# Fetching four more weight pieces and the second group's inputs in the first burst, and reordering VectorE's part of the first chain

## Chip, cores and metric

The kernel runs on one core of a Trainium2 chip. The metric is the device time of one execution in microseconds (us). A core has TensorE (PE, matrix multiply, with its weight loads shown as PEld), VectorE (DVE), ScalarE (ACT), GpSimd (POOL) and SyncE (SP), which here issues every DMA transfer.

## What is computed

Two stages follow each other. The first is a delta rule, token by token, for 4 x 8 heads of 768 tokens of size 48; the second a gated MLP on the 3072 rows that come out of it, each of 384 numbers, with 1536 hidden units:

```python
for t in range(S):
    kt, vt, bt = (k_n[:, :, t], v[:, :, t], beta[:, :, t, None])
    y[:, :, t] = np.einsum('bhd,bhde->bhe', q[:, :, t], state)
    v_old = np.einsum('bhde,bhd->bhe', state, kt)
    state = state + bt[:, :, :, None] * np.einsum('bhd,bhe->bhde', kt, vt - v_old)
...
gate = 1.0 / (1.0 + np.exp(-(x @ w_gate)))
val = x @ w_val
return (gate * val @ w_out).astype(np.float32)
```

The rows of k are normalised to length one first (k_n). The weights come as doubles, so each of their numbers arrives as two 32-bit words.

## The kernel before

The 768 tokens are cut into 12 groups of 64 tokens. For a group all 32 heads are worked at once: products of the keys among themselves (`gram`), a triangular solve by VectorE (`norms`, then `solve` or `solve_halves`), the group's share of the state (`rest`, `updates`, `advance`), masked products of keys and queries (`masked`), and the group's rows of y (`rows`), turned so that they can go into the MLP (`flip`, later `turn`). The MLP of a group is 12 tiles of 128 hidden units: `gate_val`, `gated`, `outp`. The MLP of one group runs while the delta rule of the next is prepared, in slots whose order a hand-written plan sets: the order in which instructions are written is the order in which each engine runs its own.

The first group has no MLP to run beside. Its work stands in lines 667 to 726 and is called the first chain here: on VectorE the norms of group 0, a solve in two halves of 16 steps (39 steps of `halves0`), then 11 steps of `norms1` while TensorE and ScalarE join the halves, the last two steps (the second ends in the subtraction of line 430, kept as `joint`), and then `updates(0, 0)`, `updates(0, 1)`, `updates(0, 2)`, `rows(0)` and `flip`. An `updates` step is 64 small matmuls (line 477, or 469 for the middle step) and copies out of PSUM by ScalarE (line 483) and VectorE (line 481), or two subtractions on VectorE (line 457) in the middle step. Between them `busy_array` puts filling matmuls. The first MLP matmul (line 583) is the first of slot 0.

The weights are 36 pieces of 384 KB. `load_piece` issues one (line 172); ScalarE turns the words of a piece in two passes (`scaled`, lines 189 and 191); VectorE joins them (`join`, line 203). Fourteen pieces (EAGER) are asked for by hand with `stage`: ten right away, pieces 10 and 11 once `joint` is done, 12 and 13 once ScalarE has done `lower_left(1)`. From then on `scaled(n)` asks for piece n + BEHIND when it is done. The same places also hold the loads of group 1's queries (`load_q(1)`, two transfers of 256 KB), of its keys by token (`load_rows(1, 0)`, 384 KB), and of the keys of group 2 (`load_k(2)`, two of 192 KB), whose buffer is free after the matmuls of `masked(0)`.

SP issues in the order written, and an issue that has to wait holds all behind it. Transfers complete on eight counters used in turn, so an issue also waits until the transfer eight before it has landed; at most eight are under way.

`masks0` are four VectorE multiplications (line 324) that mask the first group's query products for `rows(0)`; `halves1` is the solve of group 1, whose first four steps (lines 383 and 386) set it up; `joins` are the joins of the pieces in order.

Of the kernel before, what the change touches and what calls it, by code (L numbers as in the profile page):

```python
# [36 lines left out]
def tokens_at(e, x):  # L37
    return 64 * e if x else 64 - 64 * e
# [17 lines left out]
def deltanet_gated_mlp(ctx: ExitStack, tc: tile.TileContext, kd, qd, kv, beta, words, out):  # L56
# [27 lines left out]
    state = [{} for _ in range(N)]  # L84

    def pace(ins, after):
        if after is not None:
            tc.add_manual_dep(ins.ins, after.ins.name, mybir.DependencyInfo(mybir.DependencyClass.Sync, mybir.DependencyReason.DATA), reason="pace")
# [7 lines left out]
    def busy_array(out, n, after=()):  # L96

        for i in range(n):
            ins = nc.tensor.matmul(out=out.rearrange("q a b -> q (a b)"), lhsT=flat[:, 0:128], rhs=flat, start=True, stop=True)
            if i < len(after):  # L100
                pace(ins, after[i])

    def load_k(g):
        for e in range(2):
            nc.sync.dma_start(kqp[g % 2][64 * e:64 * e + D, 0:2].rearrange("p s c t -> p (s c t)"), kd[g, e])

    def load_q(g, after=None):
        for e in range(2):
            ins = nc.sync.dma_start(kqp[g % 2][64 * e:64 * e + 64, 2 + e:4 + e].rearrange("p s c t -> p (s c t)"), qd[g, e])
            pace(ins, after)  # L110

    def load_rows(g, part):

        st = state[g]
        if "kv" not in st:
            st["kv"] = wk.tile([128, 2, CP, D], F32, name=f"kv_{g}", tag="kv", bufs=2)
        nc.sync.dma_start(st["kv"][:, part].rearrange("p c d -> p (c d)"), kv[g, :, part * CP * D:(part + 1) * CP * D])
        if part:
            st["beta"] = wk.tile([128, 32], F32, name=f"beta_{g}", tag="beta", bufs=2)
            nc.sync.dma_start(st["beta"], beta[:, g])  # L120
# [48 lines left out]
    def load_piece(n, after=None):  # L169
        f, w = pieces[n]  # L170
        raw[n] = wt.tile([128, PW, 2], U32, name=f"raw_{n}", tag=f"w{n}")
        ins = nc.sync.dma_start(raw[n].rearrange("p c w -> p (c w)"), words[3 * f + "gvo".index(w)])
        pace(ins, after)

    def stage(lo, hi, after=None):
        for n in range(lo, hi):
            load_piece(n, after)
# [43 lines left out]
    def joining():  # L221
        for n in range(len(pieces)):
            join(n)
            yield

    def splitting():
        for n in range(len(pieces) + 1):
            if n:
                weight_lo(n - 1)
            if n < len(pieces):  # L230
                weight_hi(n)
            yield
# [78 lines left out]
    def masked(g):  # L311

        kq = kqp[g % 2]
        pool, tag = (ps_aux, "aux") if g else (ps_out, "po")
        pp = [pool.tile([128, J, C], F32, name=f"pp_{g}_{e}", tag=tag) for e in range(2)]
        for j in range(J):
            for e, x in KINDS:
                r, t = 64 * e, tokens_at(e, x)
                nc.tensor.matmul(out=pp[e][t:t + 64, j], lhsT=kq[r:r + D, x, j], rhs=kq[r:r + D, 3 if x else 2 + 2 * e, j], start=True, stop=True)  # L319

        def masks():
            for e, x in sorted(KINDS):
                t, sec = tokens_at(e, x), 5 if x else 2 + 2 * e
                nc.vector.tensor_tensor(out=kq[t:t + 64, sec], in0=pp[e][t:t + 64],  # L324
                                        in1=pmask[t:t + 64, e].unsqueeze(1).to_broadcast([64, J, C]), op=ALU.mult)
                yield
        return masks()
# [27 lines left out]
    def lower_left(g):  # L355

        if g == 0:
            for r in range(4):
                q, o = slice(32 * r, 32 * r + 32), 32 * (r % 2)
                nc.scalar.activation(wide[q, :, o:o + 16].rearrange("q c t -> q t c"), state[g]["G"][q, 0:16], AF.Copy, scale=under[q])  # L360
            return
        a = joints[g][:, 0]
        return nc.scalar.activation(a[:, :, 0:16].rearrange("q c t -> q t c"), state[g]["G"][:, 0:16], AF.Copy, scale=under)
# [5 lines left out]
    def clear(g):  # L369
        state[g]["X"] = X = wk.tile([128, 16, 32], F32, name=f"X_{g}", tag="X", bufs=1)  # L370
        nc.gpsimd.memset(X, 0.0)
# [62 lines left out]
    def rest(g):  # L434

        st = state[g]
        kq, V = kqp[g % 2], st["kv"][:, 1]
        st["pk"] = pk = [ps_seq.tile([128, J, D], F32, name=f"pk_{g}_{e}", tag="seq") for e in range(2)]
        if g == 0:
            for e in range(2):  # L440
                nc.tensor.matmul(out=pk[e].rearrange("q j d -> q (j d)"), lhsT=flat[:, 0:128], rhs=su[:, 2].rearrange("q j d -> q (j d)").bitcast(BF16)[:, 0:J * D],
                                 start=True, stop=True, skip_group_check=True)
        for j in range(J if g else 0):
            for e, x in KINDS:
                r, t = 64 * e, tokens_at(e, x)
                nc.tensor.matmul(out=pk[e][t:t + 64, j], lhsT=kq[r:r + D, x, j], rhs=su[r:r + D, 2 if x else e, j],  # L446
                                 start=j == 0, stop=True, skip_group_check=True)
        if g == 0:
            st["R"] = [V[:, e * J:(e + 1) * J] for e in range(2)]
        else:  # L450
            st["R"] = [wk.tile([128, J, D], F32, name=f"R_{g}_{e}", tag="row", bufs=3) for e in range(2)]
            less(g)

    def less(g):
        st = state[g]
        for e in range(2):
            nc.vector.tensor_tensor(out=st["R"][e], in0=st["kv"][:, 1, e * J:(e + 1) * J], in1=st["pk"][e], op=ALU.subtract)  # L457

    def updates(g, step):

        st = state[g]
        R, L = st["R"], st["L"]

        at = {(e, x): [tokens_at(e, x) + 32 * (k ^ e) for k in range(2)] for e, x in KINDS}
        if step == 1:
            for j in range(J):
                for e, x in KINDS:
                    one, two = at[e, x]
                    nc.tensor.matmul(out=st["pk"][e][two:two + 32, j], lhsT=L[one:one + 32, e * J + j], rhs=su[one:one + 32, 3 if x else e, j],  # L469
                                     start=False, stop=True, skip_group_check=True)  # L470
            less(g)
            return
        pu = [ps_aux.tile([128, J, D], F32, name=f"pu_{g}_{step}_{x}", tag="aux") for x in range(1 if g else 2)]
        for j in range(J):
            for e, x in KINDS:
                r = at[e, x][step // 2]
                nc.tensor.matmul(out=pu[0 if g else x][r:r + 32, j], lhsT=mt[r:r + 32, e * J + j], rhs=R[e][r:r + 32, j], start=True, stop=True)  # L477
        for e, x in KINDS:
            r = at[e, x][step // 2]
            if g == 0 and x:  # L480
                nc.vector.tensor_copy(out=su[r:r + 32, 3 if x else e], in_=pu[1][r:r + 32])
            else:
                nc.scalar.copy(su[r:r + 32, 3 if x else e], pu[0][r:r + 32])  # L483
# [168 lines left out]
    def take(gen, n=1):  # L652
        for _ in range(n):
            next(gen, None)
# [5 lines left out]
    scalings = [scale_v(g) for g in range(N)]  # L660
    NORMS, SOLVE, HALVES = 18, 66, 40
    joins, splits = joining(), splitting()
    EAGER, BEHIND = 14, 6


    EN = mybir.EngineType
# [6 lines left out]
    stage(3, 6)  # L673
    load_rows(0, 0)
    load_rows(1, 1)
    stage(6, 10)
    half = constants()
    clear(0)
    take(gram(0), 10)
    rest(0)  # L680
    masks0 = masked(0)
    gap.append(ps_gv.tile([128, J, C], F32, name="early", tag="gv"))
    busy_array(gap.pop(), 12)
    for n in range(2):
# [7 lines left out]
    halves0, norms1, halves1 = solve_halves(0), norms(1), solve_halves(1)  # L692
# [2 lines left out]
        scaled(n)  # L695
    take(norms1, 11)
    take(halves0, 2)
    stage(10, 12, state[0]["joint"])
    load_q(1, state[0]["joint"])
    clear(1)  # L700
    take(masks0, 2)
    updates(0, 0)
    busy_array(gap[0], 5)
    stage(12, 14, lower_left(1))
    load_rows(1, 0)
    load_k(2)
    for n in range(6, 9):
        scaled(n)
    take(masks0, 2)
    updates(0, 1)  # L710
    busy_array(gap[0], 4)
    take(norms1, NORMS)
    updates(0, 2)
    busy_array(gap[0], 5)
    for n in range(9, 11):
        scaled(n)
    take(joins, 2)
    take(halves1, 4)
    rows(0)
    busy_array(gap[0], 2)  # L720
    for n in range(11, 13):
# [6 lines left out]
    for n, at in enumerate((0, 0, 1, 2, 3, 5, 6, 8, 9, 10, 10, 11, 11, 12, 12, 13, 14, 15, 16, 16, 17, 18, 18), 13):  # L728
        plan[at].append(lambda n=n: scaled(n))
    spread(joins, len(pieces) - 4, 0, 20)  # L730
    for at, n in ((0, 8), (1, 4), (2, 6), (3, 4), (4, 5), (5, 5), (6, 1), (9, 1), (11, 1)):
        plan[at].append(steps(halves1, n))
    plan[10].insert(0, steps(halves1))
    late[10].append(steps(halves1))
# [147 lines left out]
```

## Time and profile before

| what | value |
|---|---|
| median of 3 runs | 637.5 us (637.04 to 637.57) |
| the profiled execution | 635.61 us |
| its span, first to last instruction | 633.9 us |
| TensorE busy | 614.6 us (97%) |
| VectorE busy | 476.8 us (75%) |
| ScalarE busy | 344.0 us (54%) |
| start of the first MLP matmul | 42.09 us |

The profiled execution lies 1.9 us below the median of the runs, and 1.7 us of it lie outside its span. All times of rows are counted from the span's start. On the page, the chain of work that ended last says which engine sets the end, and the timelines say when each piece ran; a wait that the trace ties to nothing is called "issue".

### The profile page before, as it was taken

How to read it: one execution, taken by the hardware profiler on the slowest of the kernel's cores; microseconds unless marked ns; L12 is line 12 of the kernel's file. 1: busy time of each engine (PE TensorE's matmuls, PEld its weight loads, DVE VectorE, ACT ScalarE, POOL GpSimd, SP SyncE). 2: the span in 40 equal slices, each digit the busy share in tenths (PEclk: the TensorE clock that was granted, in tenths of full speed). 3: DMA queues.
4: the chain of work that ended last, by engine and by line, in shares of the span. 5: the costliest groups of instructions: out<-in, count | busy, mean ns of one | idle time of the engine just before them, and what ended most of it. 6: DMA issues, size and time to landing. Idle time of an engine off the chain costs nothing.

```text
span 633.9 us, 24057 instructions
## 1 busy us (share of the span) xinstructions
PE 614.6 (97%) x10494; PEld 571.2 (90%) x10502; DVE 476.8 (75%) x1443; ACT 344.0 (54%) x933; POOL 39.6 (6%) x102
## 2 busy tenths in 40 slices
PE   6689999999999999999999999999999999999996
PEld 4367778989999999999999999999999999999996
DVE  5888897589977977977977977977987977953221
ACT  4879865567356356356355355355455455445222
POOL 6000000000002002002002002002002002001000
PEclk9999999999999999999999999999999999999999
DMA  9495831202203203103102102102112100100101
GB/s 271 177 296 181 277 91 54 53 2 87 52 3 86 52 4 86 42 12 86 45 11 86 34 21 87 27 28 86 26 29 86 26 4 3 26 3 2 26 1 25
DMA packets 17769, 41.06 MB, mean 65 GB/s; under 512 B 4224, under 2 KB 7296, under 8 KB 17664
## 3 DMA queue, kind: packets, MB, share of 16 engines
q1 hardware_dynamic: 17664, 39.53, 21.5%
q8 instruction: 82, 1.34, 0.9%
q14 instruction: 23, 0.19, 0.1%
HBM read 34.80 MB, written 4.72 MB: 62 GB/s over the span
## 4 chain that ended last, share of the span: by engine, by line
PE 91%; DVE 5%; ACT 1%; issue 1%; DMA 1%; ACTq 0%; SPq 0%; DVEq 0%
PE gv L586 45%; PE po L617 22%; PE gv L583 5%; PE pu L477 3%; PE po L611 3%; PE yy L503 2%; PE yy L506 2%; PE pk L446 2%; PE pg L291 2%; PE pp L319 2%; PE pd L524 2%; PE pk L469 1%; PE pm L409 1%; ACT su L483 1%; DVE kqp L324 1%
## 5 line engine op out<-in xcount | busy, mean ns | idle before, releaser
L586 PE MATMUL gv<-xx,w 128*128 128x256 f32 x2376 | 311.2, 285 | 0.0
L586 PEld LDWEIGHTS gv<-xx,w 128*128 128x128 f32 x2376 | 298.8, 191 | 3.1
L617 PE MATMUL po<-w,h 128*128 128x384 f32 x792 | 161.9, 340 | 0.0
L617 PEld LDWEIGHTS po<-w,h 128*128 128x128 f32 x792 | 133.8, 188 | 0.8
L597 ACT CAST h<-sg 128x256 fp32r<-128x256 f32 x132 | 53.5, 405 | 120.1 <-DVE sg L592 119.0
L591 ACT ACTIVATE sg<-gv 128x256 f32<-128x256 f32 x144 | 54.7, 380 | 107.8 <-PE gv L586 98.5
L592 DVE TENSOR_TENSOR sg<-sg,gv 128x256 f32<-128x256 f32 x144 | 60.1, 417 | 67.3 <-ACT sg L591 66.5
L350 DVE TENSOR_TENSOR X<-X,tmp 128x126 f32<-128x126 f32 (+22 forms) x279 | 71.1, 255 | 8.3
L347 DVE TENSOR_TENSOR tmp<-X,gp 128x126 f32<-128x126 f32 (+22 forms) x279 | 71.0, 254 | 8.3
L602 DVE TENSOR_TENSOR h<-sg,h 128x256 fp32r<-128x256 f32 x132 | 56.4, 428 | 13.2 <-ACT h L597 13.2
L562 POOL COPY x<-yt 32x192 f32<-32x192 f32 x72 | 28.3, 393 | 450.3 <-DVE yt L557 447.6
L279 ACT ACTIVATE kv<-kv,mq 128x48 f32<-128x48 f32 x192 | 47.9, 324 | 0.0
L483 ACT COPY su<-pu 32x384 f32<-32x384 f32 x92 | 43.3, 470 | 5.9 <-PE pu L477 4.1
L583 PE MATMUL gv<-xx,u 128*128 128x256 f32 x144 | 33.8, 385 | 0.7 <-issue 0.4
L324 DVE TENSOR_TENSOR kqp<-pp,pmask 64x512 f32<-64x512 f32 x48 | 32.3, 687 | 2.1 <-PE pp L319 1.1
L303 ACT COPY G<-pg 32x256 f32<-32x256 f32 (+1 forms) x69 | 25.3, 367 | 14.0 <-PE pg L291 12.7
L583 PEld LDWEIGHTS gv<-xx,u 128*128 128x128 f32 x144 | 26.6, 190 | 5.8 <-issue 0.8
L557 DVE STREAM_TRANSPOSE yt<-ys 128x768 f32<-128x768 f32 x9 | 8.8, 979 | 25.4 <-ACT ys L512 25.4
L457 DVE TENSOR_TENSOR R<-kv,pk 128x384 f32<-128x384 f32 x44 | 22.3, 549 | 6.6 <-PE pk L469 6.5
L562 ACT COPY x<-yt 32x192 f32<-32x192 f32 x72 | 25.2, 349 | 1.2
L212 ACT CAST w<-u 128x384 fp32r<-128x384 f32 x36 | 18.0, 508 | 8.1 <-DVE w L219 8.0
L531 DVE TENSOR_TENSOR su<-su,pd 48x384 f32<-48x384 f32 x40 | 21.7, 543 | 0.8 <-PE pd L524 0.4
(109 smaller groups left out, 556.2 us busy)
## 6 DMA issues: line engine op xcount, KB each, us to landing
raw<-in_words_dram SPq DMA_DIRECT2D x36, 384.0 KB, 5.5
kv<-in_kv_dram SPq DMA_DIRECT2D x24, 384.0 KB, 4.5
kqp<-in_qd_dram SPq DMA_DIRECT2D x24, 256.0 KB, 4.1
kqp<-in_kd_dram SPq DMA_DIRECT2D x24, 192.0 KB, 3.5
out_dram<-ot SPq DMA_DIRECT2D x48, 96.0 KB, 2.2
beta<-in_beta_dram SPq DMA_DIRECT2D x12, 16.0 KB, 4.0
```

The lines of the kernel that those rows point to most:

```text
L279: nc.scalar.activation(V[:, c], V[:, c], AF.Copy, scale=mq[:, c, 0:1])
L347: nc.vector.tensor_tensor(out=tmp, in0=X[:, k:16, j:j + 1].to_broadcast([128, n, j]), in1=gp[:, j:j + 1, 0:j].to_broadcast([128, n, j]), o ...
L350: nc.vector.tensor_tensor(out=X[:, k:16, 0:j], in0=X[:, k:16, 0:j], in1=tmp, op=ALU.add)
L483: nc.scalar.copy(su[r:r + 32, 3 if x else e], pu[0][r:r + 32])
L562: copy(x[32 * q:32 * q + 32, :, :, a].rearrange("q k c s -> q c k s"), yt[32 * a:32 * a + 32, :, q::4])
L583: nc.tensor.matmul(out=pg[:, o], lhsT=parts[w, f][:, k * 128:(k + 1) * 128], rhs=x[0][:, k], start=k == 0, stop=k == KC - 1)
L586: nc.tensor.matmul(out=pg[:, o], lhsT=parts[w, f][:, a, k * 128:(k + 1) * 128], rhs=x[b][:, k], start=(k == 0 and q == 0), stop=(k == KC - ...
L591: nc.scalar.activation(h, st["gv", f][:, 0], AF.Sigmoid)
L592: nc.vector.tensor_tensor(out=h, in0=h, in1=st["gv", f][:, 1], op=ALU.mult)
L597: nc.scalar.copy(hh[:, 0], st["sg", f])
L602: nc.vector.tensor_tensor(out=hh[:, 1], in0=st["sg", f], in1=hh[:, 0].bitcast(F32), op=ALU.subtract)
L617: nc.tensor.matmul(out=po[s], lhsT=hh[:, a, ts], rhs=parts["o", f][:, w], start=(f == 0 and q == 0), stop=(f == NF - 1 and q == 2))
```

## The change

- Pieces 10 to 13, the queries of group 1 and its keys by token are asked for right behind the first ten pieces, with no wait for `joint` or `lower_left(1)`; the keys of group 2 right behind `masked(0)`.
- BEHIND falls from 6 to 5: `scaled(n)` asks for piece n + 5, so piece 14 is asked for by `scaled(9)`, no longer by `scaled(8)`.
- The first two joins move from before `rows(0)` to before `updates(0, 0)`.
- The last two masks move from before `updates(0, 1)` to behind it.
- The last seven steps of `norms1` move from before `updates(0, 2)` to behind it.
- The first four steps of `halves1` move from before `rows(0)` into slots 1 to 3.

```diff
--- before.py
+++ after.py
@@ -660,7 +660,7 @@
     scalings = [scale_v(g) for g in range(N)]
     NORMS, SOLVE, HALVES = 18, 66, 40
     joins, splits = joining(), splitting()
-    EAGER, BEHIND = 14, 6
+    EAGER, BEHIND = 14, 5
 
 
     EN = mybir.EngineType
@@ -673,12 +673,15 @@
     stage(3, 6)
     load_rows(0, 0)
     load_rows(1, 1)
-    stage(6, 10)
+    stage(6, 14)
+    load_q(1)
+    load_rows(1, 0)
     half = constants()
     clear(0)
     take(gram(0), 10)
     rest(0)
     masks0 = masked(0)
+    load_k(2)
     gap.append(ps_gv.tile([128, J, C], F32, name="early", tag="gv"))
     busy_array(gap.pop(), 12)
     for n in range(2):
@@ -695,27 +698,22 @@
         scaled(n)
     take(norms1, 11)
     take(halves0, 2)
-    stage(10, 12, state[0]["joint"])
-    load_q(1, state[0]["joint"])
     clear(1)
     take(masks0, 2)
+    take(joins, 2)
     updates(0, 0)
     busy_array(gap[0], 5)
-    stage(12, 14, lower_left(1))
-    load_rows(1, 0)
-    load_k(2)
+    lower_left(1)
     for n in range(6, 9):
         scaled(n)
-    take(masks0, 2)
     updates(0, 1)
     busy_array(gap[0], 4)
-    take(norms1, NORMS)
+    take(masks0, 2)
     updates(0, 2)
     busy_array(gap[0], 5)
+    take(norms1, NORMS)
     for n in range(9, 11):
         scaled(n)
-    take(joins, 2)
-    take(halves1, 4)
     rows(0)
     busy_array(gap[0], 2)
     for n in range(11, 13):
@@ -728,7 +726,7 @@
     for n, at in enumerate((0, 0, 1, 2, 3, 5, 6, 8, 9, 10, 10, 11, 11, 12, 12, 13, 14, 15, 16, 16, 17, 18, 18), 13):
         plan[at].append(lambda n=n: scaled(n))
     spread(joins, len(pieces) - 4, 0, 20)
-    for at, n in ((0, 8), (1, 4), (2, 6), (3, 4), (4, 5), (5, 5), (6, 1), (9, 1), (11, 1)):
+    for at, n in ((0, 8), (1, 6), (2, 7), (3, 5), (4, 5), (5, 5), (6, 1), (9, 1), (11, 1)):
         plan[at].append(steps(halves1, n))
     plan[10].insert(0, steps(halves1))
     late[10].append(steps(halves1))
```

## Rows read from the trace of the kernel before

**Rows 1.** The page of the profiled execution: its first part (busy time, share of the span and instructions of each engine), one queue of its third part (packets, MB, share of 16 DMA engines), and the shares by engine in its fourth part, the chain of work that ended last.

```profile
PE 614.6 (97%) x10494; PEld 571.2 (90%) x10502; DVE 476.8 (75%) x1443; ACT 344.0 (54%) x933; POOL 39.6 (6%) x102
...
q8 instruction: 82, 1.34, 0.9%
...
PE 91%; DVE 5%; ACT 1%; issue 1%; DMA 1%; ACTq 0%; SPq 0%; DVEq 0%
```

**Rows 2.** The timeline of TensorE's matmuls from the span's start to 75 us: start and duration of a run of like instructions, line, operation, tiles and shapes, count, and in brackets the idle time before it with what ended it.

```profile
26.53 1.50 PE L409 MATMUL pm<-scratch 32*32 32x32 f32 x128 [0.35 <-ACT scratch L423]
...
28.82 0.86 PE L477 MATMUL pu<-kv,mt 32*32 32x48 f32 x59
30.99 0.28 PE L477 MATMUL pu<-kv,mt 32*32 32x48 f32 x5 [1.31 <-issue]
...
32.39 0.99 PE L469 MATMUL pk<-su,L 32*32 32x48 f32 x64
...
38.39 1.14 PE L506 MATMUL yy<-su,kqp 128*64 128x48 f32 x32
...
40.51 0.85 PE L542 MATMUL pt<-ident,ys 128*128 128x128 f32 x6 [0.44 <-ACT raw L191]
...
42.09 5.42 PE L583 MATMUL gv<-xx,u 128*128 128x256 f32 x24 [0.31 <-DVE xx L545]
...
71.64 1.13 PE L583 MATMUL gv<-xx,u 128*128 128x256 f32 x4 [0.42 <-issue]
```

**Rows 3.** Stretches that begin and end at chosen instructions of TensorE: length; then for each of the five engines the busy time and, after the x in brackets, the number of instructions that ran in it (those cut by an edge count too); granted clock, DMA share, GB/s.

```profile
30.98:71.63 40.65, 37.93 (x761) 28.79 (x765) 35.10 (x105) 35.52 (x90) 0.52 (x1) 1.00 0.79 248
30.98:35.55 4.57, 3.86 (x127) 2.40 (x130) 4.02 (x10) 4.23 (x9) 0.00 (x0) 1.00 1.00 283
23.69:30.98 7.29, 5.44 (x254) 4.31 (x256) 5.88 (x15) 5.12 (x14) 0.52 (x1) 1.00 0.17 44
23.69:27.07 3.38, 2.92 (x126) 2.62 (x128) 3.14 (x9) 2.18 (x8) 0.52 (x1) 1.00 0.02 5
8.92:23.69 14.77, 11.43 (x139) 5.11 (x136) 13.01 (x56) 11.86 (x32) 2.04 (x5) 1.00 0.88 307
```

**Rows 4.** The DMA view of six stretches of 0.1 us, one row each, in this order: 12.9 to 13.0, 24.9 to 25.0, 28.3 to 28.4, 33.0 to 33.1, 42.7 to 42.8 and 69.2 to 69.3 us. Each holds the start of one packet of the queue that brings instructions: packets, MB, and the packet's whole time as a share of 16 engines in that 0.1 us (70.9% of 1.6 us is 1.13 us).

```profile
q8 instruction: 1, 0.02, 70.9%
q8 instruction: 1, 0.02, 61.9%
q8 instruction: 1, 0.02, 69.1%
q8 instruction: 1, 0.02, 74.7%
q8 instruction: 1, 0.02, 68.4%
q8 instruction: 1, 0.02, 63.9%
```

**Rows 5.** Four stretches of 2 us, columns as in the third group; the last three columns are the granted TensorE clock, the busy share of the 16 DMA engines and the GB/s that they moved.

```profile
8.00:10.00 2.00, 1.74 (x63) 1.69 (x62) 1.86 (x3) 1.90 (x6) 1.81 (x6) 1.00 1.03 399
16.00:18.00 2.00, 0.22 (x1) 0.19 (x2) 1.74 (x8) 1.90 (x5) 0.00 (x0) 1.00 1.04 390
26.00:28.00 2.00, 1.65 (x130) 1.32 (x130) 1.61 (x8) 2.00 (x5) 0.00 (x0) 1.00 0.00 0
36.00:38.00 2.00, 1.52 (x19) 0.73 (x22) 1.87 (x6) 1.99 (x5) 0.00 (x0) 1.00 0.88 259
```

**Rows 6.** SP's queue, three views: its timeline (six issues of pieces, from the first one's start over the wait among them to the end of the last); the DMA issued in the stretch from 8.2 to 8.4 us (line and tiles, count, KB, us from issue to landing); and of SP's waits (us in total, times, longest) the one on the first chain's last subtraction.

```profile
12.33 17.46 SPq L172 DMA_DIRECT2D raw<-in_words_dram  x6
...
raw<-in_words_dram SPq DMA_DIRECT2D x1, 384.0 KB, 9.2
...
SPq L172 <- DVE mt L430: 11.2, 1, 11.2
```

**Rows 7.** The timeline of VectorE (DVE), columns as in the second group.

```profile
28.80 1.39 DVE L324 TENSOR_TENSOR kqp<-pp,pmask 64x512 f32<-64x512 f32 x2
31.32 1.14 DVE L481 COPY su<-pu 32x384 f32<-32x384 f32 x2 [1.13 <-PE pu L477]
32.49 1.40 DVE L324 TENSOR_TENSOR kqp<-pp,pmask 64x512 f32<-64x512 f32 x2
33.92 1.02 DVE L457 TENSOR_TENSOR kv<-kv,pk 128x384 f32<-128x384 f32 x2
...
36.50 1.14 DVE L481 COPY su<-pu 32x384 f32<-32x384 f32 x2
37.67 1.03 DVE L203 SCALAR_TENSOR_TENSOR u<-raw 128x384 uint32<-128x384 uint32 x2
...
39.80 0.56 DVE L510 COPY ys<-yy 128x384 f32<-128x384 f32 x1
```

**Rows 8.** The timeline of ScalarE (ACT), columns as in the second group.

```profile
34.99 0.55 ACT L191 ACTIVATE raw<-raw 128x384 f32<-128x384 f32 x1
...
39.11 0.48 ACT L512 COPY ys<-yy 128x384 f32<-128x384 f32 x1 [0.43 <-PE yy L506]
...
41.29 0.46 ACT L545 COPY xx<-pt 128x384 f32<-128x384 f32 x1
...
44.99 0.56 ACT L189 ACTIVATE raw<-raw 128x384 int32<-128x384 uint16 x1 [2.35 <-DMA raw<-in_words_dram]
```

## The prediction

> **What bounds the kernel now.** I read the page's busy shares and its chain of work first: TensorE is busy for 97% of the span and carries 91% of the chain that ended last [rows 1]. So a time can only change where TensorE stands still. The timeline of its matmuls shows where: almost only before 42.09 us, where the first MLP matmul starts; behind that it runs nearly without a break, and what moves this start moves the end by as much [rows 2]. Everything in the change lies ahead of that point or takes load off the time behind it.
>
> Two idle times of TensorE in these rows are put down to "issue", that is, to nothing the profile shows: 1.31 us inside the 64 small matmuls of `updates(0, 0)`, which stop after 59 and go on at 30.99 us, and 0.42 us inside a row of MLP matmuls that go on at 71.64 us [rows 2]. Next I counted instructions. The queue that brings instructions moved 82 packets of 16 KB for TensorE's 10494 + 10502 instructions, 256 to a packet [rows 1]. Between the two stops lie 761 + 765 = 1526 instructions, six times 254 [rows 3], so both stand on the edge of such a block. And in front of each lies a packet: one starts at 28.3 us, takes 1.1 us and is followed by the restart 1.6 us after its end; one starts at 69.2 us, takes 1.0 us, restart 1.4 us after its end [rows 4]. I read both as TensorE waiting for its own next block of instructions.
>
> When is a block asked for? Counting back from 30.98 us, 254 instructions lie between 23.69 and 27.07 us and 510 between 23.69 and 30.98 us [rows 3]. So blocks begin at 23.7, 27.1 and 31.0 us, and the packet for the next block starts 1.2 us after 23.7 (at 24.9) and 1.2 us after 27.1 (at 28.3) [rows 4]: a block is asked for when the one before it begins. In those stretches the DMA engines move nothing [rows 5]. Where they are full, the packet comes later: the block that begins at about 8.9 us (a block's count back; 275 with those cut by the edges) has its packet at 12.9, 4.05 us later, at 399 GB/s; the one that begins at 31.0 at 33.0, 2.05 us; the one at 35.55 (257 instructions on) at 42.7, 7.2 us, at 259 GB/s around it [rows 3 to 5].
>
> Now the block that begins at 27.07 us. Its packet starts at 24.9, takes 1.0 us, and 1.4 us later it is 27.3: this block is ready just as TensorE gets to it. There is no slack, and it lies inside the 128 matmuls of line 409 (26.53 to 28.03 us), on the first chain [rows 2 to 4].
>
> **The change part by part. The transfers.** In the kernel before, SP has issued piece 9 by about 16.5 us and at 17.5 us (8.29 + 9.2, the landing of a piece issued eight transfers earlier) it stops for `joint`, for 11.2 us [rows 6]. From 22 to 28 us the DMA engines therefore have nothing to move, which is what gives the blocks of 24.9 and 28.3 us their short way [rows 4, 5]. The change takes this pause out: 4 pieces, 2 x 256 KB of queries, 384 KB of keys by token and 2 x 192 KB of keys follow at once, 2816 KB or 2.9 MB. At 390 GB/s [rows 5] that is 7.4 us, so the DMA engines stay full from 21.5 to about 29 us, and by the rule of eight transfers in flight SP keeps eight of them queued at 23.7 us, as at 8.9 us. The packet that TensorE asks for at 23.7 us comes into a full queue.
>
> Its delay does not stand in the trace of before. The bounds are 2.05 us (at 31.0, when SP had been issuing again for two us only) and 7.2 us (at 35.55, with queries and keys among the queued, by the order of the code, and only about 259 GB/s); with a short queue 1.2 us would stay. I take 4.05 us, the row at 8.9 us: eight transfers queued, the engines at almost 400 GB/s, as they are with pieces. Then the packet starts at 23.7 + 4.05 = 27.75, ends at 28.85, and TensorE gets the block at 28.85 + 1.4 = 30.25 in place of 27.25 us: **+3.0 us**, all of it on the chain, since line 430 on VectorE, `updates(0, 0)` and all else wait for these matmuls. With the bounds it is +1.0 and +6.2 us. The next block, asked for at 30.25, finds the queue nearly empty; its 1.2 + 1.1 + 1.6 us give again the stop of 1.3 us inside `updates(0, 0)`, moved along. It could be up to 0.8 us longer if the last transfers are still queued (2.05 for 1.2 us). Later blocks have either more time or, behind 30 us, less traffic than before.
>
> **Piece 14 and BEHIND.** ScalarE's one wait for a piece, 2.35 us before 44.99 us, goes away [rows 8], since the queue ahead of piece 14 is gone. It was hidden: TensorE ran through it [rows 2]. Nothing is gained, and with 5 pieces ahead nothing is lost, unless a piece then comes later than ScalarE wants it; the slots give pieces several us.
>
> **VectorE's order.** All times here are those of before; the delay above adds to them.
> - Two masks (1.39 us) and now two joins (1.03 us) follow the subtraction that ends at 28.77, so VectorE is free at 31.2 us. The copies of `updates(0, 0)` start at 31.32 us, after the stop for instructions [rows 2, 7]. The joins cost nothing, with 0.1 us of cover; without that stop they would cost 1.0 us.
> - The other masks (1.40 us) no longer stand in front of line 457. Its matmuls are done at 33.4 us (32.39 + 0.99), the masks ended at 33.9, so line 457 starts 0.4 us earlier, at 33.5 [rows 2, 7].
> - VectorE then does line 457 (1.02 us, to 34.5), the masks (to 35.9), the copies of `updates(0, 2)` (1.14 us, to 37.05, 0.6 us earlier than before). The seven norm steps (1.56 us between 34.94 and 36.50) follow and end at 38.6 [rows 7].
> - `rows(0)` so ends at 38.5 instead of 39.1 us (38.39 + 1.14, with half a matmul's overlap), and with it ScalarE's copy at 39.11 comes at 38.5 [rows 2, 8]. ScalarE is free by then: its passes for pieces 6 to 8 still end at 35.54, and the two copies and two pieces behind them fit.
> - VectorE's half of that copy came at 39.80 us because the joins and four `halves1` steps stood in front of it [rows 7]; now it can start at 38.6 and end at 39.2. The transposes (0.85 us) follow at 39.3 instead of 40.5.
> - Behind ScalarE's copy still stand two pieces (four passes) and then the copy of line 545, 41.29 + 0.46 = 41.75 us before, 41.1 us now [rows 8]. VectorE's copy ends at 40.7. ScalarE is now the last, and the first MLP matmul can start at about 41.2 instead of 42.09 us: **-0.85 us**. Of the 1.2 us that VectorE gains, ScalarE's passes hold back a third.
> - The four steps moved into slots 1 to 3 (about 1.1 us) fall where VectorE waits for TensorE and ScalarE; cost nothing.
>
> Sum: +3.0 - 0.85 = +2.15 us, a span of 636.05 us and an execution of 637.8 us against 635.6. The median of the runs lies 1.9 us above the profiled execution: 637.5 + 2.15 = **639.6 us**.
>
> **Rivals.** (a) The blocks of instructions are not held up, because the packet of 24.9 us is not bound to the data queues as I think: only the reordering counts, -0.85 us, 636.6 us. For it: the link rests on three delayed packets. Against it: both unexplained stops stand on a block's edge behind a packet. The point from which it decides: at a delay of 1.2 + 0.85 = 2.05 us the sum is zero, and below that the kernel is not slower.
> (b) The packet is let in early among the data: the trace's quickest under full load is the 2.05 us at 31.0, so +1.0 - 0.85 = +0.15 us, 637.6 us. [...]
> (c) The queue with queries and keys is as slow as at 35.55: 7.2 us, +6.2 - 0.85 = +5.35 us, 642.8 us. For it: the same kinds of transfers stand in the queue. Against: four plain pieces go first.
> (d) The standing TensorE loses its clock. At 16 to 18 us it did 0.22 us of work in 2 us and kept a granted clock of 1.00 [rows 5]; a stop of 3 us is longer than any such stretch there. [...]
>
> **How the numbers follow.** Forecast, delays of about 3.3 to 6 us (638.8 to 641.5 us): 0.50. (c) 0.14. (d) 0.07. (b) 0.12. (a) 0.13. Another mishap 0.04. The range runs from (a), 636.4, to just over (c), 643.0 us, and leaves out the worse half of (d) and mishaps. A measurement of this kernel can tell 0.2%, 1.3 us, from no change: slower is above 638.8, faster below 636.2 us. The forecast, (c) and (d) lie above, with a tenth of the forecast's cases at the edge counted as the same: slower 0.66. (a) and (b) lie within: same 0.28. Faster, if (a) comes with more from the reordering than I see: 0.06.
>
> **What would show it.** Right: an idle time of TensorE of about 3 us, put down to "issue", inside the matmuls of line 409, with an instruction packet that starts near 27.7 instead of 24.9 us; DMA engines full from 21.5 to 29 us; the first MLP matmul near 44.2 us; ScalarE's copy of line 545 as the last before it. Wrong: line 409 runs through, the packet starts by 25.5 us, and the first MLP matmul comes at 41 to 42 us; or the stop is there and the time behind 42 us gives it back.

## The result and the profile after

| | kernel before | kernel changed |
|---|---|---|
| median | 636.02 us (8 runs, 634.63 to 637.57) | 639.48 us (8 runs, 638.31 to 640.65) |
| profiled execution | 635.61 us, span 633.9 us | 640.65 us, span 639.0 us |
| first MLP matmul | 42.09 us | 47.54 us |

The ratio is 1.0052, with a 95% interval of 1.0036 to 1.0067: the changed kernel is slower by 3.5 us (2.3 to 4.3 us). The five further runs of the kernel before lie lower than the three shown first, so its median is 636.0 and not 637.5 us; the 639.6 us forecast fell on the measured 639.48 us partly for that reason. The forecast difference was +2.15 us, the measured one +3.46 us. The profiled execution of the changed kernel is the slowest of its eight.

TensorE's timeline of the changed kernel, against [rows 2]:

```profile
26.53 0.74 PE L409 MATMUL pm<-scratch 32*32 32x32 f32 x62
31.39 1.16 PE L409 MATMUL pm<-scratch 32*32 32x32 f32 x66 [4.12 <-issue]
...
33.87 1.48 PE L477 MATMUL pu<-kv,mt 32*32 32x48 f32 x59
35.66 0.37 PE L477 MATMUL pu<-kv,mt 32*32 32x48 f32 x5 [0.31 <-issue]
35.97 2.31 PE L99 MATMUL gap<-dmask 128*128 128x512 bf16 x5
38.21 1.50 PE L469 MATMUL pk<-su,L 32*32 32x48 f32 x64
...
47.54 5.42 PE L583 MATMUL gv<-xx,u 128*128 128x256 f32 x24 [0.31 <-ACT xx L545]
```

The 128 matmuls of line 409 ran through in the kernel before. Now they stop after 62 for 4.12 us, put down to "issue", and go on at 31.39 us. The stop inside line 477 has shrunk from 1.31 to 0.31 us, because the matmuls before it run slower: these 59 take 1.48 us instead of 0.86. The next two views say why the stop is there. First, stretches between the chosen instructions, as in [rows 3]:

```profile
23.69:31.38 7.69, 3.33 (x128) 2.71 (x128) 3.82 (x12) 6.06 (x18) 0.53 (x1) 0.88 1.04 282
31.38:35.66 4.28, 3.97 (x128) 2.60 (x128) 3.00 (x5) 0.00 (x0) 0.00 (x0) 0.50 0.35 90
```

Both hold 128 + 128 instructions: 31.39 and 35.66 us are again edges of blocks of 256, and the one at 31.39 us is the edge that stood at 27.07 us before. Then two stretches of 0.1 us of the DMA view, from 28.6 and from 33.3 us, each with the start of one packet of instructions, as in [rows 4]:

```profile
q8 instruction: 1, 0.02, 81.2%
...
q8 instruction: 1, 0.02, 64.1%
```

The packet that started at 24.9 us now starts at 28.66 us, takes 1.3 us (81.2% of 1.6 us) and is followed by the restart 1.4 us after its end. The one behind it starts at 33.3 us and ends 1.3 us before 35.66 us. Stretches of 2 us, with granted clock, DMA share and GB/s at the end of each row, against [rows 5]:

```profile
22.00:24.00 2.00, 1.68 (x13) 0.64 (x14) 1.75 (x6) 2.00 (x9) 0.22 (x1) 1.00 1.01 387
26.00:28.00 2.00, 1.13 (x64) 0.62 (x62) 1.61 (x8) 2.00 (x5) 0.00 (x0) 1.00 1.10 276
28.00:30.00 2.00, 0.00 (x0) 0.00 (x0) 0.00 (x0) 1.93 (x5) 0.00 (x0) 0.87 1.03 237
30.00:32.00 2.00, 0.61 (x46) 0.61 (x49) 0.00 (x0) 0.00 (x0) 0.00 (x0) 0.50 1.00 215
32.00:34.00 2.00, 2.00 (x49) 0.82 (x42) 1.38 (x2) 0.00 (x0) 0.00 (x0) 0.50 0.41 114
38.00:40.00 2.00, 2.00 (x67) 1.54 (x67) 0.18 (x1) 2.00 (x6) 0.00 (x0) 0.57 0.00 0
```

Where the DMA engines moved nothing from 26 to 28 us they are full until about 33 us, at first with 387 GB/s, later with no more than 215 to 276. And TensorE's clock, which stayed at 1.00 in these stretches before, is at 0.50 from about 29.5 to 39.7 us: it fell during the stop. VectorE and ScalarE, against [rows 7, 8]:

```profile
36.08 1.14 DVE L481 COPY su<-pu 32x384 f32<-32x384 f32 x2 [0.45 <-PE pu L477]
39.82 1.02 DVE L457 TENSOR_TENSOR kv<-kv,pk 128x384 f32<-128x384 f32 x2 [2.60 <-issue]
...
45.25 0.56 DVE L510 COPY ys<-yy 128x384 f32<-128x384 f32 x1 [0.28 <-PE yy L506]
```

```profile
46.94 0.47 ACT L545 COPY xx<-pt 128x384 f32<-128x384 f32 x1
```

The order is the new one: line 457 (39.82 us) runs ahead of the masks (the next line of VectorE's timeline, at 40.76 us), and VectorE's part of the copy out of `rows(0)` (45.25 us) follows its ScalarE half by half a microsecond instead of lagging by 0.7 us. ScalarE's copy of line 545 ends at 47.41 us and lets the MLP start.

### The profile page after: what moved, and what is told of

Its sections match the earlier page's. It is cut to its first block, busy times and chain, and to the rows that moved or that the text cites. A ratio compares the mean times of both kernels' runs of the same rounds, so it can differ in the third digit from the quotient of the medians.

```text
span 639.0 us, 24063 instructions
## 1 busy us (share of the span) xinstructions
PE 618.4 (97%) x10502; PEld 572.7 (90%) x10502; DVE 476.7 (75%) x1443; ACT 344.2 (54%) x933; POOL 40.0 (6%) x102
## 4 chain that ended last, share of the span: by engine, by line
PE 90%; DVE 5%; ACT 2%; issue 2%; DMA 1%; ACTq 0%; SPq 0%; DVEq 0%
PE gv L586 44%; PE po L617 21%; PE gv L583 5%; PE pu L477 3%; PE po L611 3%; PE yy L503 2%; PE yy L506 2%; PE pk L446 2%; PE pg L291 2%; PE pp L319 2%; PE pd L524 1%; PE pk L469 1%; PE pm L409 1%; ACT su L483 1%; DVE kqp L324 1%
## 5 line engine op out<-in xcount | busy, mean ns | idle before, releaser
L562 POOL COPY x<-yt 32x192 f32<-32x192 f32 x72 | 28.7, 399 | 450.0 <-DVE yt L557 447.3
```

Of the source, the lines that this page charges most:

```text
L562: copy(x[32 * q:32 * q + 32, :, :, a].rearrange("q k c s -> q c k s"), yt[32 * a:32 * a + 32, :, q::4])
```

## The experiments

Each ratio is to runs of the kernel before on the same chip at the same time; their medians were 635.4 to 635.7 us. A ratio is worked out over all runs of both kernels and need not equal the quotient of the two medians.

**The transfers alone.** The kernel before with the transfers of the change and BEHIND 5, VectorE's order left alone:

```diff
-    stage(6, 10)
+    stage(6, 14)
+    load_q(1)
+    load_rows(1, 0)
...
     masks0 = masked(0)
+    load_k(2)
...
-    stage(10, 12, state[0]["joint"])
-    load_q(1, state[0]["joint"])
...
-    stage(12, 14, lower_left(1))
-    load_rows(1, 0)
-    load_k(2)
+    lower_left(1)
```

> The kernel before with the transfers of the change alone (pieces 10 to 13, queries and keys of group 1 in the first burst, keys of group 2 behind masked(0), BEHIND 5) and VectorE's order as before. Theory (TensorE's next block of instructions waits behind the full DMA queue): a stop of 3 to 4 us inside line 409, a lower clock behind it, 3 to 5 us slower than before. Rival (the new order of VectorE costs the time): within 0.7 us of before.

Measured: 639.96 us, ratio 1.0066 (1.0043 to 1.0089). TensorE's timeline:

```profile
31.77 1.17 PE L409 MATMUL pm<-scratch 32*32 32x32 f32 x66 [4.51 <-issue]
...
46.39 5.42 PE L583 MATMUL gv<-xx,u 128*128 128x256 f32 x24 [0.31 <-DVE xx L545]
```

The DMA view of the 0.1 us from 29.0 us:

```profile
q8 instruction: 1, 0.02, 76.6%
```

The stop is there, 4.51 us long, without any change on VectorE. The transfers alone make up the whole loss.

**The order alone.** The changed kernel with the transfers put back to where they were before (the diff above with its signs turned round), and with BEHIND:

```diff
-    EAGER, BEHIND = 14, 5
+    EAGER, BEHIND = 14, 6
```

> VectorE's order of the change alone, all transfers and BEHIND as before. Theory: no stop in line 409, the stop of 1.3 us inside line 477 stays, first MLP matmul at 41.2 us, 0.85 us faster than before. Rival (the order costs): 3 us slower or more.

Measured: 634.82 us against 635.4, ratio 0.9998 (0.9979 to 1.0017): no difference that can be told. TensorE's timeline:

```profile
26.80 1.29 PE L409 MATMUL pm<-scratch 32*32 32x32 f32 x128 [0.36 <-ACT scratch L423]
...
30.98 0.28 PE L477 MATMUL pu<-kv,mt 32*32 32x48 f32 x5 [1.24 <-issue]
...
36.35 0.37 PE L477 MATMUL pu<-kv,mt 32*32 32x48 f32 x14 [1.15 <-issue]
...
42.17 5.42 PE L583 MATMUL gv<-xx,u 128*128 128x256 f32 x24 [0.31 <-ACT xx L545]
```

The DMA view of the 0.1 us from 33.5 us:

```profile
q8 instruction: 1, 0.02, 78.4%
```

Line 409 runs through, so the order does not cost what the change costs. But the MLP starts at 42.17 us and not at 41.2. The second run of line 477 now stops after 50 matmuls for 1.15 us, until 36.35 us: the next edge of a block (257 instructions after 30.98 us before, [rows 3]). In the kernel before TensorE came to this edge at 35.55 us, just when the block came. Here it comes 0.35 us earlier, at 35.20 us, and the block comes 0.8 us later: its packet starts at 33.54 us, not at 33.05. So in this execution the gain turns into a wait for instructions; why the packet came later is not shown. The twelve runs spread widely, seven from 633.8 to 635.0 us and five from 636.5 to 638.4 us, and what the longer ones wait for was not profiled.

**The edges moved.** The changed kernel, with 60 instructions more behind the gram products of group 1:

```diff
-    busy_array(gap.pop(), 12)
+    early = gap.pop()
+    busy_array(early, 12)
...
-    take(gram(1), 10)
+    copies1 = gram(1)
+    for i in range(30):
+        nc.tensor.matmul(out=early.rearrange("q a b -> q (a b)")[:, 0:32], lhsT=flat[:, 0:128], rhs=flat[:, 0:32], start=True, stop=True)
+    take(copies1, 10)
```

> The changed kernel with 30 small filling matmuls (60 instructions with their loads) behind the gram products of group 1, where TensorE is idle. Theory: every edge of a block of instructions moves 60 instructions earlier in the program, so the block asked for at 23.7 us is asked for at about 16 us and is there in time; line 409 runs through, and the stop moves to the next edge, inside line 477, where it lasts 2 to 4 us instead of 1.3. Joining the halves ends at 28.8 us again; the whole 1 to 2 us faster than the changed kernel. Rival (full DMA engines slow or stop TensorE's reads at that time, whatever the instruction): the stop stays inside line 409.

Measured: 644.19 us, ratio 1.0138 (1.0116 to 1.0161), slower than the changed kernel and not faster. TensorE's timeline, and the DMA view of the 0.1 us from 31.4 us:

```profile
26.57 1.29 PE L409 MATMUL pm<-scratch 32*32 32x32 f32 x128 [0.36 <-ACT scratch L423]
...
28.65 0.53 PE L477 MATMUL pu<-kv,mt 32*32 32x48 f32 x29
34.32 1.01 PE L477 MATMUL pu<-kv,mt 32*32 32x48 f32 x35 [5.15 <-issue]
...
75.76 0.37 PE L409 MATMUL pm<-scratch 32*32 32x32 f32 x18 [2.83 <-issue]
```

```profile
q8 instruction: 1, 0.02, 80.7%
```

The stop has left line 409 and stands in line 477, after 29 matmuls, where an edge moved by 60 instructions must lie (59 matmuls and 30 fewer). The data that the DMA engines moved was the same; only the place of the edges differed. That decides against slow reads or any wait for data of line 409. The size was wrong, 5.15 us instead of 2 to 4: the block asked for at 26.8 us got its packet at 31.4 us. And the shift moved the edges of the whole program, where one now costs 2.83 us at 75.8 us.

**All of it at the end of the solve.** The changed kernel, the held-back transfers asked for when line 430 is done:

```diff
-    stage(6, 14)
-    load_q(1)
-    load_rows(1, 0)
+    stage(6, 10)
...
-    load_k(2)
...
     take(halves0, 2)
+    stage(10, 14, state[0]["joint"])
+    load_q(1, state[0]["joint"])
+    load_rows(1, 0)
+    load_k(2)
```

> The changed kernel, but pieces 10 to 13, the queries and keys of group 1 and the keys of group 2 asked for at the end of the first chain's solve (line 430), without the wait for lower_left(1); BEHIND 5. Theory: the DMA engines are idle at 23.7 us again, so no stop in line 409 and a full clock: as order_only, 0.85 us faster than before and 4.3 us faster than the changed kernel. Rival (BEHIND 5 or the missing wait for lower_left costs): slower than order_only by 1 us or more.

Measured: 637.56 us, ratio 1.0029 (1.0011 to 1.0047), its twelve runs lie between 635.1 and 640.0 us. The profiled execution took 635.3 us; its timeline of TensorE has no stop in line 409, but one in the second run of line 477:

```profile
35.97 0.37 PE L477 MATMUL pu<-kv,mt 32*32 32x48 f32 x14 [0.87 <-issue]
```

So the expectation failed: 2.2 us slower instead of 0.85 faster. Nine transfers are asked for from 28.7 us on, and the stop ends at 35.97 us: with the 1.2 us that such a packet took elsewhere and the 1.4 us from its end to a restart, the packet for the edge at 30.9 us started near 33.4 us (an estimate). What the longer executions wait for was not profiled and stays open.

**All of it later.** The same, but asked for after lower_left(1), at 33 us:

```diff
-    lower_left(1)
+    done1 = lower_left(1)
+    stage(10, 14, done1)
+    load_q(1, done1)
+    load_rows(1, 0)
+    load_k(2)
```

> VectorE's order of the change, and pieces 10 to 13, queries and keys of group 1 and keys of group 2 all asked for only when ScalarE has done lower_left(1), at about 33 us; BEHIND 5. Theory: the DMA engines are idle at 23.7, 27.1 and 31.0 us, so all three packets of instructions come on the short way: no stop in line 409, 1.3 us in the first run of line 477, and none in the second one (0.9 to 1.2 us in the two runs with transfers from 28.8 us on). First MLP matmul at 40.9 to 41.2 us, 0.9 us faster than before, and 0.5 us faster than order_only. Rival (the second stop in line 477 does not come from the transfers): it stays, and the time is that of order_only.

Measured: 638.59 us, ratio 1.0042 (1.0029 to 1.0055). TensorE's and ScalarE's timelines:

```profile
34.19 1.11 PE L477 MATMUL pu<-kv,mt 32*32 32x48 f32 x64
...
41.07 5.42 PE L583 MATMUL gv<-xx,u 128*128 128x256 f32 x24 [0.31 <-ACT xx L545]
...
49.52 2.86 PE L583 MATMUL gv<-xx,u 128*128 128x256 f32 x12 [1.22 <-DVE sg L592]
...
69.61 1.36 PE L409 MATMUL pm<-scratch 32*32 32x32 f32 x128 [1.87 <-DVE scratch L422]
```

```profile
47.75 0.56 ACT L189 ACTIVATE raw<-raw 128x384 int32<-128x384 uint16 x1 [4.99 <-DMA raw<-in_words_dram]
```

Half of it holds: the second run of line 477 has all 64 matmuls without a stop, and the MLP starts at 41.07 us, the 1.0 us that the order was worth. But ScalarE waits 4.99 us for piece 14, TensorE waits for gated values (1.22 us at 49.5 us) and later for VectorE (1.87 us at 69.6 us). So there is a latest time for the pieces, too: asked for with queries and keys among them at 33 us, they come too late to stay hidden.

**Only the pieces early.** The changed kernel with queries and keys held back:

```diff
     stage(6, 14)
-    load_q(1)
-    load_rows(1, 0)
...
-    load_k(2)
...
-    lower_left(1)
+    load_q(1, lower_left(1))
+    load_rows(1, 0)
+    load_k(2)
```

> The changed kernel with the four pieces in the first burst, but the queries and keys of group 1 and the keys of group 2 only after lower_left(1). The transfers then end at 25.4 us, two pieces being left in the queue at 23.7. Theory: the packet starts as those end, at 25.3 to 25.8 instead of 24.9 us, the stop in line 409 is 0.5 to 1.2 us, no half clock, and the whole within 0.6 us of before. Rival (any transfer in the queue holds the packet for 4 us or more): a stop of 3 us or more.

Measured: 635.76 us, ratio 1.0008 (0.9998 to 1.0019). TensorE's timeline, and the DMA view of the 0.1 us from 25.9 us:

```profile
28.46 0.86 PE L409 MATMUL pm<-scratch 32*32 32x32 f32 x66 [1.19 <-issue]
...
30.65 1.64 PE L477 MATMUL pu<-kv,mt 32*32 32x48 f32 x64
...
42.17 5.42 PE L583 MATMUL gv<-xx,u 128*128 128x256 f32 x24 [0.31 <-ACT xx L545]
```

```profile
q8 instruction: 1, 0.02, 75.1%
```

The stop is 1.19 us, the packet starts at 25.9 us. Fewer bytes ahead of it, a shorter delay: 2.2 us from 23.7 us instead of 5. (The transfers held back are also of another kind; this run does not part number of bytes and kind.) The half clock came against the expectation, and line 477 without a stop took 1.64 us. A stretch of 2 us, the granted clock third from the end:

```profile
30.00:32.00 2.00, 2.00 (x64) 1.35 (x64) 1.96 (x5) 0.00 (x0) 0.00 (x0) 0.50 0.00 0
```

**BEHIND alone.** The kernel before with one number changed:

```diff
-    EAGER, BEHIND = 14, 6
+    EAGER, BEHIND = 14, 5
```

> The kernel before with BEHIND 5 alone (pieces 14 to 35 asked for one piece later). Theory: nothing, within 0.6 us of before; ScalarE's wait for piece 14 grows by up to 2 us, hidden behind TensorE. Rival (pieces come too late or move the later stops for instructions): 1 us slower or more.

Measured: 635.83 against 635.64 us, ratio 0.9999 (0.9982 to 1.0016): no difference, as forecast. ScalarE's wait for piece 14 did not grow, though: its timeline has none. TensorE's timeline, and a stretch of 2 us:

```profile
36.54 0.37 PE L477 MATMUL pu<-kv,mt 32*32 32x48 f32 x14 [0.94 <-issue]
```

```profile
20.00:22.00 2.00, 2.00 (x5) 0.42 (x4) 1.72 (x9) 1.96 (x8) 0.00 (x0) 0.50 1.01 390
```

Both show how much an execution can differ without the change. The stop in the second run of line 477 is here too, with VectorE's old order. And the clock is at 0.50 from 20 to 22 us, ahead of any of these stops. In the profile of the kernel before it was 1.00 there, after a wait of 1.86 us for VectorE that ended at 17.78 us.

**The changed kernel once more.** No edit; it is run for a second profile.

> The changed kernel once more, for a second profile. Theory: the instruction packet asked for at 23.7 us starts at 28 to 29 us, the stop in line 409 is 3.3 to 4.2 us, the clock falls to half behind it for some 7 to 10 us, and the whole is 3 to 5 us slower than before. Rival (the 4.1 us of the first profile came from the slow first transfers of that one execution): a stop under 2.5 us and no half clock.

Measured: 639.44 us, ratio 1.0062 (1.0042 to 1.0083). Its timeline of TensorE, and the DMA view of the 0.1 us from 28.7 us:

```profile
31.44 1.17 PE L409 MATMUL pm<-scratch 32*32 32x32 f32 x66 [4.18 <-issue]
...
33.93 1.62 PE L477 MATMUL pu<-kv,mt 32*32 32x48 f32 x64
...
45.44 5.42 PE L583 MATMUL gv<-xx,u 128*128 128x256 f32 x24 [0.31 <-ACT xx L545]
```

```profile
q8 instruction: 1, 0.02, 80.8%
```

A stop of 4.18 us, the packet at 28.8 us, a half clock from about 28.8 until about 35.6 us, the end of which lies in this stretch:

```profile
35.00:36.00 1.00, 1.00 (x27) 0.62 (x17) 1.00 (x3) 0.48 (x2) 0.00 (x0) 0.70 0.00 0
```

This second profile separates two things that the first one mixed, as the next section uses.

**Without the fillers.** The changed kernel without the 17 filling matmuls between the solve's last product and `rows(0)`; they compute nothing that the output needs:

```diff
-            busy_array(gap[0], 3)
...
     updates(0, 0)
-    busy_array(gap[0], 5)
...
     updates(0, 1)
-    busy_array(gap[0], 4)
...
     updates(0, 2)
-    busy_array(gap[0], 5)
```

> The changed kernel without the 17 filling matmuls between the end of the solve and rows(0) (3, 5, 4 and 5). Theory: behind the stop the clock is at half, where five fillers last 1.3 to 2.3 us instead of 1.03 and delay the small matmuls behind them; without them the first MLP matmul comes 0.5 to 1.5 us earlier after the stop. Rival (the fillers are what brings the clock back): the half clock lasts into the MLP, and the whole is 1 us or more slower than the changed kernel.

Measured: 641.89 us, ratio 1.0101 (1.0084 to 1.0117), against 1.0052 and 1.0062 for the changed kernel. The rival held. A stretch of 2 us:

```profile
44.00:46.00 2.00, 1.67 (x27) 1.28 (x24) 0.64 (x2) 1.50 (x4) 0.00 (x0) 0.50 0.85 226
```

The clock is still at 0.50 from 44 to 46 us, where both profiles of the changed kernel had it back by 39.7 us. The fillers do cost time at half clock, but without them the half clock lasts longer and costs more. (The 34 instructions that are gone also move the later edges, so not all of the difference need be the clock's.)

**The transfers spread.** The changed kernel with this:

```diff
-    EAGER, BEHIND = 14, 5
+    EAGER, BEHIND = 14, 6
...
-    stage(6, 14)
-    load_q(1)
-    load_rows(1, 0)
+    stage(6, 12)
...
     masks0 = masked(0)
-    load_k(2)
...
-    lower_left(1)
+    stage(12, 14, lower_left(1))
+    load_k(2)
...
+    plan[4].append(lambda: load_rows(1, 0))
+    plan[5].append(lambda: load_q(1))
     plan[13].append(lambda: load_q(2))
```

> VectorE's order of the change with BEHIND 6 and the transfers spread out: pieces 10 and 11 in the first burst (they are done at 23.4 us), 12 and 13 and the keys of group 2 after lower_left(1) at 33 us, the keys and queries of group 1 only in slots 4 and 5. Theory: the DMA engines are idle at 23.7, 27.1 and 31.0 us, so there is no stop in line 409 and none in the second run of line 477; and pieces 12 to 14 come in time for ScalarE, so TensorE does not wait for gated values as it did with all of them asked for at 33 us. First MLP matmul at 41.1 us, the whole 0.7 to 1.0 us faster than before, 4 us faster than the changed kernel. Rival (the late queries and keys only move the queue onto later packets of instructions): a new stop of 1 us or more behind 42 us, within 0.5 us of before.

Measured: 634.42 against 635.67 us, ratio 0.9978 (0.9966 to 0.9990), faster than both kernels. TensorE's timeline:

```profile
26.51 1.37 PE L409 MATMUL pm<-scratch 32*32 32x32 f32 x128 [0.35 <-ACT scratch L423]
...
30.84 0.28 PE L477 MATMUL pu<-kv,mt 32*32 32x48 f32 x5 [1.31 <-issue]
...
34.12 1.11 PE L477 MATMUL pu<-kv,mt 32*32 32x48 f32 x64
...
40.99 5.42 PE L583 MATMUL gv<-xx,u 128*128 128x256 f32 x24 [0.31 <-ACT xx L545]
```

Line 409 and the second run of line 477 run through, the stop of 1.31 us in the first run is the old one, and the MLP starts 1.1 us earlier than before and is not held up behind that. This 1.1 us is the gain that VectorE's order had in it, close to the 1.0 us with all transfers later. The span is 1.8 us shorter than before, and of the rest 0.4 us is the stop of [rows 2] at 71.64 us, which is not there. The expected 0.7 to 1.0 us lie within the measured 0.6 to 2.2 us.

## Why the prediction was right, and where its sizes were off

**The place and the cause held.** The stop came in line 409, at the edge of a block of instructions, with the packet late and the DMA engines full. The transfers alone bring it, the order alone does not, edges moved by 60 instructions take it along, and fewer bytes in the queue make it shorter. The 128 + 128 instructions between 31.38 and 35.66 us agree with 256 to a packet. That a block is asked for when the one before it begins remains my reading of the times between edges and packets; no view shows the request itself.

**The delay of the packet was mis-sized.** I took 4.05 us from the row at 8.9 us and got 30.25 us for the restart. The packet asked for at 23.7 us started at 28.66 and 28.8 us in the two profiles, 5.0 and 5.1 us later, and itself took 1.3 us instead of the 1.1 us set. So the stop was 4.1 to 4.2 us and not 3.0. The term that was off is the delay, by the choice of its row: "the engines at almost 400 GB/s, as they are with pieces". The 399 GB/s hold for 8 to 10 us only [rows 5]. Over the whole delay in the kernel before, and over the delays in the two profiles of the changed kernel, the rows are:

```profile
8.90:12.97 4.07, 3.74 (x58) 2.25 (x54) 3.63 (x14) 2.57 (x6) 2.06 (x5) 1.00 1.04 303
23.70:28.66 4.96, 3.33 (x128) 2.71 (x128) 3.81 (x12) 4.78 (x16) 0.53 (x1) 1.00 1.04 310
23.70:28.78 5.08, 3.33 (x128) 2.71 (x128) 3.80 (x12) 3.86 (x12) 0.52 (x1) 1.00 1.05 284
```

The mean rate is much the same, 303 against 310 and 284 GB/s, although it fell late in the delay, when queries and keys followed the pieces. What differs is how much was moved ahead of the packet: 1.2 MB there, 1.5 and 1.4 MB here. In the row of the other bound, 35.55 to 42.79 us, it is 1.9 MB at 263 GB/s. What sets this amount stays open; eight transfers queued do not fix it. The DMA engines were not done at 29 us: from 30 to 32 us their share was 1.00 in the first profile and 0.75 in the second, from 32 to 34 us 0.41 and 0.16.

**Rival (b)** fares badly: with eight transfers queued the packet waited 5 us in both profiles, and 2.2 us with most of these transfers held back.

**Rival (d) came true beside the forecast**, where I had given it 0.07 as a case of its own. In the profile of the kernel before the clock was 1.00 in every stretch read behind 16 us [rows 3, 5]; that was true of one execution. With BEHIND 5 alone it was 0.50 from 20 to 22 us, and from 22 to 24 us its mean was 0.96 with only the pieces early and 0.93 without the fillers. With the stop in line 409 the clock fell to half in both profiles of the changed kernel, for about 10.2 us in the first and 6.8 us in the second. Up to the end of the first run of line 477 it cost next to nothing: from the edge in line 409 to there the second profile took 35.55 - 31.44 = 4.11 us, the kernel before, at full clock but with its stop of 1.31 us, 31.27 - 27.07 = 4.20 us. The slower matmuls fill the wait for the next block, which I had expected to be a stop again. What a longer half clock cost can be read from the two profiles. From the end of the first run of line 477 to the first MLP matmul the kernel before took 42.09 - 31.27 = 10.82 us [rows 2]. The second profile, with the clock back by 35.6 us, took 45.44 - 35.55 = 9.89 us: 0.93 us less, which is the order's -0.85 us (0.95 us in the run with the transfers spread, 40.99 - 31.12 = 9.87 us, without any half clock there). The first took 47.54 - 36.03 = 11.51 us: with the same order, 1.6 us more, all of it in the half clock, above all in the five fillers (2.31 us for 1.29 in the second profile) and line 469 (1.50 us for 0.96). What (d) would cost, which the range and the chances use, is shown by no run and was my estimate; the runs showed these 1.6 us for the longer half clock.

**The sum.** Second profile: the first run of line 477 ends 4.28 us later than before, the order takes back 0.93, so the MLP starts 3.35 us later; the span is 2.7 us longer. First profile: 4.76 - 0.93 + 1.6 = 5.4 us, the span 5.1 us longer. The medians, 3.5 and 3.8 us, lie between. The forecast was 3.0 - 0.85. The start of the MLP does not quite move the end by as much, as I had put it; in the second profile, for one, the stop of 0.42 us at 71.64 us [rows 2] has no counterpart.

**VectorE's order** was priced rightly where the next block of instructions comes in time: 0.93 to 1.1 us for the 0.85. Alone it shows no gain in the mean. In its one profile TensorE meets the edge at which the block had come just in time before, and the block comes 0.8 us later. I had noted such a just-in-time edge at 27.07 us and had not looked at the one at 35.55 us in the same way.

**Piece 14 and BEHIND** cost and bring nothing, as forecast: ScalarE's wait for piece 14 is gone and the time does not follow. The reason I gave is not shown: with BEHIND 5 alone, and the transfers as before, the wait is gone from the profile too.

## What to carry to other kernels

Count TensorE's instructions in stretches of many small matmuls. Here two stops that the profile ties to nothing, 1.31 us in line 477 of the kernel before and 4.12 us in line 409 of the changed one, each stood on an edge of 256. The packet of instructions in front of the first started 1.2 us after the edge before, with the DMA engines moving nothing [rows 2 to 5]; the one in front of the second started 5.0 us after it, with the DMA engines moving 310 GB/s. In this kernel an empty DMA queue was worth more than early data: 634.42 us with the transfers spread, 639.48 us with all of them in the first burst. So try to ask for what is not due soon only when the next blocks of instructions have come, and to spread it out. When a step is made faster, look at what is just in time behind it, instructions included.

## What the runs showed of the hardware

- A packet of 16 KB of instructions started 1.2 us after the edge at which I take it to be asked for, with idle DMA engines [rows 3 to 5]. It started 2.2 us after it with the last 0.8 MB of pieces still to move (23.7 to 25.9 us, at 399 GB/s up to 24 us and a mean of 346 GB/s from 24 to 26 us). In three profiles with all transfers early and the edge at 23.7 us it started 5.0, 5.1 and 5.35 us after it (28.66 and 28.78 us in the two of the changed kernel, 29.05 us in the run with the transfers alone).
- Behind a stop of TensorE of 4.1 to 4.5 us the granted clock was 0.50 in all four profiles where it was read (both of the changed kernel, the transfers alone, and without the fillers). By the means of stretches of 2 us it fell at 28.3 to 29.5 us and came back 6.8, 6.8 and 10.2 us later in the three with the fillers; without them it was still 0.50 almost 17 us after it fell (29.1 to 46 us). I had expected this in one case of fourteen. A stop of 4 us was not needed: the clock also fell to 0.50 behind the stop of 1.19 us, and with BEHIND 5 alone it was 0.50 from 20 to 22 us, where in the profile of the kernel before, after a wait of 1.86 us, it stayed at 1.00.
